# Linear attention, softplus MLP and routed experts on one Trainium2 core: later weight-rest matmuls in an expert unit, and weight conversions held behind attention steps

## The chip, the cores and the metric

One core of one Trainium2 chip. The metric is the device time of one execution in microseconds (us). Engines: PE (TensorE), DVE (VectorE), ACT (ScalarE), POOL (GpSimd), and SP, whose queue issues most DMAs.

## The reference

Three layers in a row, all in float32.

```
q_p, k_p = phi(q), phi(k)                 # phi(x) = exp(x@omega.T - |x|^2/2 - max) / sqrt(m), x scaled
out = (q_p @ (k_p.T @ v)) / (q_p @ sum(k_p) + 1e-6)     # 4 batches, 8 heads, 576 rows, head 64, m = 128
x   = out as 2304 tokens x 512
x   = softplus(x @ w_in) @ w_out          # 512 -> 2048 -> 512
e   = argmax(cosine(x, expert_emb) / tau)  # 8 experts, one per token
out = gate * (relu(x @ w1[e]) @ w2[e])    # 512 -> 1024 -> 512
```

## The kernel before

**Attention** runs in steps (lists `steps` and `loads`, 20 steps for each of 4 batches). Step t transposes one item of q or k (`stage_T`, lines 262 to 270), one step later projects it and takes the exponential (`stage_P`, 282 to 301), and after a lag folds it into the key-value sums (`stage_K`, 318) or turns it for the output (`stage_Q`, 365 to 377). `stage_N`, `stage_M` and `stage_X` (395 to 444) form the quotient and write x. PE, DVE and ACT each have several short instructions in every step. The loads of q and k are issued on SP four steps ahead, those of v one step ahead.

**The MLP** handles 2304 tokens in 6 groups of 384, and d_ff = 2048 in 16 chunks. A chunk is `mm1` (line 638, x times a column block of w_in), the softplus chain on ACT and DVE (653 to 668), and `mm2` (703, times a row block of w_out). Group 0 takes the weights in plain fp32, a chunk's two products in one fp32 matmul each; later groups split each operand into a rounded high part and a rest (fp32r) and make three passes: high by high, rest by high, high by rest. Group 0 starts when attention's first 30 steps are traced (`need[0]=30`); the remaining steps are interleaved with the MLP.

**Weight conversion.** The MLP's weights are loaded in 32 tiles of 512 KB (`load_w`, lines 536 and 540, even n from w_in, odd n from w_out) and turned into scaled values by three DVE instructions each (`conv_ops`, lines 558, 561 and 564). Tiles pass through three staging slots: two of tag `wst`, shared with some router temporaries, and one (`wst3`) for every third tile. `load_w(n + 2)` is called before tile n is converted. `mm1` of chunk f needs tile 2f, `mm2` of chunk f needs tile 2f+1.

**What sets the order.** Up to the first expert unit a planner orders each engine's queue when the kernel is built, from program order and from when it reckons operands and buffers are ready; work that is traced later may so come earlier where an engine would stand idle. On the chip each queue runs in that order. `tc.issue_after(ins)` ties the instructions traced in its block to follow `ins`, on the engine of `ins` alone; here that is DVE, so the loads on SP are not tied. In the kernel before, the loop over the first 30 steps sets the mark only in step 0 (`conv_gate=0`), never converts early (`conv_early=99`), and then calls `conv_to(5)`:

```
    while cur[0] < TUNE["need"][0]:
        if cur[0] >= TUNE["conv_early"] and done_w[0] < 3:
            conv_to(3)
        next(micro)
        if cur[0] <= TUNE["conv_gate"] and traced().engine == mybir.EngineType.DVE:
            marks["conv"] = traced()
    with tc.issue_after(marks["conv"]) if "conv" in marks else ExitStack():
        conv_to(TUNE["conv_first"])
```

**Experts.** Tokens are gathered by expert in slots of 128. A unit (`unit`) is one slot ("single") or two slots with the same expert ("pair"): four singles, then six turns of a pair and a single, then one more single. From unit 1 on the order is written out by hand (`manual_schedule`). While a unit runs, the next one's w1 is split, chunk by chunk c = 0 to 3 (`unit_w1`): ACT writes the high part (line 1246), DVE the rest (line 1250). A single's first product is in two halves of 512 columns (`slot_m1`, line 1336, 12 matmuls of 512 columns each, x stationary); a pair's in four parts k (`pair_m1`, line 1358, 24 matmuls of 256 columns each, w1 stationary). `PASSES` gives the order inside a chunk: high x by high w, high x by rest of w, rest of x by high w. The second product is line 1370.

Of the kernel before, what the change touches and what calls it, by code (L numbers as in the profile page):

```python
# [50 lines left out]
    v_ahead=1,  # L51
    setup=2,
    conv_first=5,
    conv_gate=0,
    conv_early=99,
    gap=0,
    rate=140,
    man=1,
    order='XMTNnKPZ',
# [17 lines left out]
def tile_kernel(ctx, tc, q, k, v, omega, w_in, w_out, emb, tau, w1, w2, out):  # L77
    nc = tc.nc
# [9 lines left out]
    NC = DM // P  # L88
# [1150 lines left out]
    def split(hi, lo, lo_eng, src, relu=False, hi_eng="a"):  # L1239
        if relu:  # L1240
            nc.scalar.activation(out=hi, in_=src, func=AF.Relu)
            nc.vector.scalar_tensor_tensor(out=lo, in0=src, scalar=0.0, in1=hi.bitcast(F32),
                                           op0=ALU.max, op1=ALU.subtract)
        else:
            if hi_eng == "a":
                nc.scalar.copy(out=hi, in_=src)  # L1246
            else:
                (nc.gpsimd if hi_eng == "p" else nc.vector).tensor_copy(hi, src)
            eng = nc.gpsimd if lo_eng == "p" else nc.vector
            eng.tensor_tensor(out=lo, in0=src, in1=hi.bitcast(F32), op=ALU.subtract)  # L1250
# [3 lines left out]
    def mpsum(use, name):  # L1254
        opts = {"t": ("tp", "tp", "kv"), "h": ("h", "pr"), "o": ("y0", "y1", "y2")}[use]
        turns[use] = turns.get(use, -1) + 1
        tag = opts[turns[use] % len(opts)]
        pool = psh if tag == "h" else psy if tag[0] == "y" else psa
        return pool.tile([P, 512], F32, tag=tag, name=name, bufs=2 if tag == "tp" else 1)

    def transposed(src, name):
        pt = mpsum("t", name)
        n = src.shape[1]
        for c in range(n):
            nc.tensor.transpose(pt[:, c * P:c * P + P], src[:, c, :], ident)
        return pt

    xs, w1s, w2s = {}, {}, {}
    PASSES = ((0, 0), (0, 1), (1, 0))

    def unit_x(g):

        n = len(groups[g])
        if n == 2:
            t = [ring.tile([P, 2, 2, P], F32R, tag=f"wi{x}", name=f"mx{x}{k}") for k in range(2) for x in "hl"]
            xs[g] = [[t[2 * (c // 2) + a][:, c % 2] for c in range(NC)] for a in range(2)]
        else:
            if g < NS_A:
                t = [ring.tile([P, NC, P], F32R, tag=f"wi{x}", name=f"mx{x}") for x in "hl"]
            else:  # L1280
                t = xpool.tile([P, 2, NC, P], F32R, tag="xlo", name="mx")
                t = [t[:, 0], t[:, 1]]
            xs[g] = [[x[:, c] for c in range(NC)] for x in t]
        for i, s in enumerate(groups[g]):
            pt = transposed(xgs[s][:, 0:DM].rearrange("t (p c) -> t c p", c=NC), "pt_x")
            pt = pt.rearrange("p (c t) -> p c t", c=NC)
            if n == 2:
                parts = [(t[2 * k][:, :, i, :], t[2 * k + 1][:, :, i, :], pt[:, 2 * k:2 * k + 2]) for k in range(2)]
                for hi, lo, src in parts:
                    nc.scalar.copy(out=hi, in_=src)  # L1290
                for hi, lo, src in parts:
                    nc.vector.tensor_tensor(out=lo, in0=src, in1=hi.bitcast(F32), op=ALU.subtract)
            else:
                split(*t, "v", pt)
# [33 lines left out]
    def slot_m1(g, half, part=slice(0, 12)):  # L1328
        if part.start == 0:
            hs["ps", half] = mpsum("h", "ph")  # L1330
        ph = hs["ps", half]
        w = slice(half * HF, half * HF + HF)
        mms = [(xs[g][a][c], w1s[g, c][b_][:, w]) for c in range(NC) for a, b_ in PASSES]
        for i in range(part.start, part.stop):
            x, r = mms[i]
            nc.tensor.matmul(ph, lhsT=x, rhs=r, start=(i == 0), stop=(i == 3 * NC - 1))  # L1336
# [14 lines left out]
    def pair_m1(g, k):  # L1351

        ph = hs["ps"] = mpsum("h", "ph")
        for c in range(NC):
            for j in range(2):
                f = slice(2 * k * P + j, 2 * (k + 1) * P, 2)
                for n, (a, b_) in enumerate(PASSES):
                    nc.tensor.matmul(ph[:, j * 256:j * 256 + 256], lhsT=w1s[g, c][b_][:, f],  # L1358
                                     rhs=xs[g][a][c].rearrange("p i t -> p (i t)"),
                                     start=(c == 0 and n == 0 and j == 0), stop=(c == NC - 1 and n == 2),  # L1360
                                     skip_group_check=True)

    def unit_m2(g, i, parts):

# [24 lines left out]
    def unit(g):  # L1389
# [22 lines left out]
        if ahead:  # L1412
            fetch_w(g + 2, "1", 1)
        if len(groups[g]) == 2:
            pair_m1(g, 0)
            own(2, 3, 4)
            split(*hidden(0), "v", hs["ps"], relu=True)
            pair_m1(g, 1)
            own(5)
            split(*hidden(1), "v", hs["ps"], relu=True)  # L1420
            pair_m2(g, 0)
            pair_m1(g, 2)
            own(6, 7)
            fetch()
# [7 lines left out]
            if nxt:  # L1432
                unit_x(g + 1)
# [4 lines left out]
        else:  # L1438
            if g > 0:
                slot_m1(g, 0)  # L1440
            own(2, 3, 4)
            slot_relu(0)
            slot_m1(g, 1, slice(0, 5))
            own(5)
            slot_t(0)
            slot_m1(g, 1, slice(5, 12))
            own(6, 7)
            slot_relu(1)
# [4 lines left out]
            if nxt:  # L1453
                unit_x(g + 1)
# [39 lines left out]


    PRE = {TUNE["pre_x"]: [lambda: unit_x(0)]}
    for c in range(NC):
        PRE.setdefault(TUNE["pre_w1"][c], []).append(lambda c=c: unit_w1(0, c))
# [5 lines left out]
    for n in range(NCH):  # L1504
        g, f = divmod(n, NF)
# [22 lines left out]
        if 0 < g < LAST:  # L1528
            t, off = divmod(f - TUNE["y_from"], TUNE["y_step"] if g < LAST - 1 else 1)
# [60 lines left out]
```

## Time and profile before

| what | value |
|---|---|
| median of 3 runs | 950.11 us (948.86 to 951.63) |
| the profiled execution | 950.99 us, span 949.1 us |
| PE busy | 895.0 us (94%) |
| DVE, ACT, POOL busy | 694.6, 651.7, 345.1 us |
| mean granted TensorE clock | 0.991 |

The span is the time from the first to the last instruction in the trace; the execution's own time is 1.9 us more. A share of busy time is a mean over stages: attention alone, attention with MLP group 0, the other MLP groups, the experts. PE's busy time also holds waits inside a matmul group, so it is an upper bound of its work.

### The profile page before, as it was taken

Reading aid. Unit: us, or ns where it says so; the run is one execution under the profiler, and the core shown is the slowest. Engines: PE = TensorE matmul, PEld = TensorE weight load, DVE = VectorE, ACT = ScalarE, POOL = GpSimd, SP = SyncE. Lnnn points to the kernel's source line nnn. Section 1 sums busy time; section 2 is a strip of 40 time slices with the busy share of each in tenths; the row PEclk is TensorE's granted clock in tenths of the full one; section 3 lists DMA queues with packets and bytes.
Section 4 is the critical chain, followed back from the end, with each engine's and each line's share of the span. In section 5 each row is a group of like instructions: output and inputs, shape, how many; then the busy total and the mean of one; then the engine's idle time right before and its main releaser. Section 6 shows DMA issues by size and latency. Waiting matters only on the chain. (4 is left out here: it accounts for less than half of the span.)

```text
span 949.1 us, 14505 instructions
## 1 busy us (share of the span) xinstructions
PE 895.0 (94%) x4951; PEld 743.6 (78%) x4951; DVE 694.6 (73%) x1376; ACT 651.7 (69%) x1452; POOL 345.1 (36%) x341
## 2 busy tenths in 40 slices
PE   7788989999999999999999999999999999999993
PEld 6666545588888879887888889887787887878872
DVE  6698875477888776689886777768967676685762
ACT  4787445477778867776777678876867576585672
POOL 1332400255446654566653110012653242252410
PEclk9999999999999999999999999999999999999997
DMA  4656660011262212010301281102114661451820
GB/s 117 188 170 199 185 180 28 12 39 37 56 147 69 48 47 71 26 40 17 67 7 23 73 331 63 34 12 57 34 56 161 253 240 70 169 211 36 324 86 6
DMA packets 86540, 94.69 MB, mean 100 GB/s; under 512 B 50294, under 2 KB 74870, under 8 KB 84160
## 3 DMA queue, kind: packets, MB, share of 16 engines
q1 hardware_dynamic: 77888, 45.21, 18.4%
q0 software_dynamic: 8576, 48.52, 13.7%
q8 instruction: 41, 0.67, 0.3%
q14 instruction: 35, 0.29, 0.1%
HBM read 108.36 MB, written 15.48 MB: 130 GB/s over the span
## 5 line engine op out<-in xcount | busy, mean ns | idle before, releaser
L1370 PE MATMUL po<-w,mh_h 128*128 128x512 f32 x368 | 116.8, 398 | 0.5 <-ACT mh_h L1347 0.5
L1385 POOL DMA_INDIRECT out_dram<-ot,s_idx x23 | 46.3, 2015 | 166.9 <-ACT ot L1384 126.0
L703 PE MATMUL y<-woh,gh 128*128 128x512 f32 x240 | 97.7, 411 | 3.2 <-DVE gh L682 3.2
L1250 DVE TENSOR_TENSOR w<-w2r,w 128x512 fp32r<-128x512 f32 x136 | 88.2, 687 | 12.3 <-ACT w L1246 12.1
L703 PE MATMUL y<-wol,gh 128*128 128x512 f32 x240 | 94.9, 398 | 0.0
L1246 ACT CAST w<-w2r 128x512 fp32r<-128x512 f32 x136 | 79.4, 643 | 18.4 <-DMA w2r<-in_moe_w_dram,w_idx 9.0
L1250 DVE TENSOR_TENSOR w<-w1r,w 128x1024 fp32r<-128x1024 f32 x68 | 80.3, 1226 | 11.2 <-ACT w L1246 11.2
L703 PE MATMUL y<-woh,gl 128*128 128x512 f32 x240 | 81.5, 406 | 0.4 <-POOL gl L683 0.4
L598 DVE TENSOR_TENSOR wil<-win,wih 128x512 fp32r<-128x512 f32 x72 | 56.9, 790 | 29.2 <-ACT wih L597 25.9
L638 PE MATMUL h<-xhi,wih 128*128 128x384 f32 x320 | 73.6, 349 | 2.8 <-DVE t L657 2.5
L1370 PEld LDWEIGHTS po<-w,mh_h 128*128 128x128 f32 x368 | 66.1, 189 | 12.2 <-ACT mh_h L1347 0.7
L1246 ACT CAST w<-w1r 128x1024 fp32r<-128x1024 f32 x68 | 71.9, 1121 | 3.8 <-PE ph L1336 2.1
L1358 PE MATMUL ph<-mxh,w 128*128 128x256 f32 x384 | 73.0, 286 | 1.4 <-DVE w L1250 0.5
L1370 PE MATMUL po<-w,mh_l 128*128 128x512 f32 x184 | 72.6, 395 | 1.7 <-DVE mh_l L1349 1.7
L425 POOL TENSOR_TENSOR xf<-xf,rc 128x256 f32<-128x256 f32 (+1 forms) x20 | 19.9, 994 | 143.7 <-ACT rc L424 129.0
L638 PE MATMUL h<-xlo,wih 128*128 128x384 f32 x320 | 71.9, 340 | 0.0
L638 PE MATMUL h<-xhi,wil 128*128 128x384 f32 x320 | 69.6, 337 | 0.0
L1358 PEld LDWEIGHTS ph<-mxh,w 128*128 128x128 f32 x384 | 62.7, 195 | 5.1 <-DVE w L1250 3.8
L610 POOL TENSOR_TENSOR wol<-wout,woh 128x512 fp32r<-128x512 f32 x40 | 54.2, 1355 | 27.8 <-ACT woh L609 24.9
L638 PEld LDWEIGHTS h<-xhi,wih 128*128 128x128 f32 x320 | 55.1, 188 | 7.6 <-DVE t L657 3.0
L638 PEld LDWEIGHTS h<-xhi,wil 128*128 128x128 f32 x320 | 57.5, 188 | 0.0
L638 PEld LDWEIGHTS h<-xlo,wih 128*128 128x128 f32 x320 | 56.5, 188 | 0.5
(311 smaller groups left out, 2415.1 us busy)
## 6 DMA issues: line engine op xcount, KB each, us to landing
wst<-in_moe_w_in_dram SPq DMA_DIRECT2D x16, 512.0 KB, 3.9
wst<-in_moe_w_out_dram SPq DMA_DIRECT2D x16, 512.0 KB, 3.7
raw<-in_k_dram SPq DMA_DIRECT2D x32, 128.0 KB, 2.3
vf<-in_v_dram SPq DMA_DIRECT2D x64, 64.0 KB, 2.2
raw<-in_q_dram SPq DMA_DIRECT2D x32, 128.0 KB, 2.3
ya<-yt SPq DMA_DIRECT2D x20, 128.2 KB, 3.9
yb<-yt SPq DMA_DIRECT2D x20, 128.2 KB, 3.6
ya<-yt SPq DMA_DIRECT2D x8, 256.5 KB, 4.7
```

The costliest lines, as they stand in the source:

```text
L425: nc.gpsimd.tensor_tensor(out=xf, in0=xf, in1=rc, op=ALU.mult)
L598: feng("il", n).tensor_tensor(out=il, in0=wi, in1=ih.bitcast(F32), op=ALU.subtract)
L610: feng("ol", n).tensor_tensor(out=ol, in0=wo, in1=oh.bitcast(F32), op=ALU.subtract)
L638: nc.tensor.matmul(h[:, 0:G], lhsT=a[:, c, :], rhs=x[:, c, :], start=(i == 0), stop=(i == last))
L703: nc.tensor.matmul(y, lhsT=x[:, c], rhs=w, start=(f == 0 and i == 0), stop=(f == NF - 1 and i == len(passes) - 1))
L1246: nc.scalar.copy(out=hi, in_=src)
L1250: eng.tensor_tensor(out=lo, in0=src, in1=hi.bitcast(F32), op=ALU.subtract)
L1358: nc.tensor.matmul(ph[:, j * 256:j * 256 + 256], lhsT=w1s[g, c][b_][:, f], rhs=xs[g][a][c].rearrange("p i t -> p (i t)"), start=(c == 0 an ...
L1370: nc.tensor.matmul(po[s], lhsT=h[a][:, o:o + P], rhs=w2s[g, c][b_], start=(c == 0 and n == 0), stop=(c == 7 and n == 2))
L1385: nc.gpsimd.indirect_dma_start(out=out, out_offset=bass.IndirectOffsetOnAxis(ap=s_idx[:, s:s + 1].bitcast(U32), axis=0), in_=ot, in_offset ...
```

## The change

Two edits. `first_order` puts, in the first half of a single's first product and in the first part of a pair's, the matmuls with the rest of w1 behind all the others; the other parts keep their order by chunk, but a pair's parts now run through the two column halves j inside a pass. And the mark is now set by every step up to 29, tiles 0 to 2 are converted from step 8 on, and tiles 3 and 4 (`conv_to(5)`) are tied to the mark.

```
-    conv_gate=0,
-    conv_early=99,
+    conv_gate=29,
+    conv_early=8,
...
+    def first_order(part):
+        if part == 0:
+            return [(c, p) for c in range(NC) for p in ((0, 0), (1, 0))] + [(c, (0, 1)) for c in range(NC)]
+        return [(c, p) for c in range(NC) for p in PASSES]
...
-        mms = [(xs[g][a][c], w1s[g, c][b_][:, w]) for c in range(NC) for a, b_ in PASSES]
+        mms = [(xs[g][a][c], w1s[g, c][b_][:, w]) for c, (a, b_) in first_order(half)]
...
-        for c in range(NC):
+        order = first_order(k)
+        for n, (c, (a, b_)) in enumerate(order):
             for j in range(2):
                 f = slice(2 * k * P + j, 2 * (k + 1) * P, 2)
-                for n, (a, b_) in enumerate(PASSES):
-                    nc.tensor.matmul(ph[:, j * 256:j * 256 + 256], lhsT=w1s[g, c][b_][:, f],
-                                     rhs=xs[g][a][c].rearrange("p i t -> p (i t)"),
-                                     start=(c == 0 and n == 0 and j == 0), stop=(c == NC - 1 and n == 2),
-                                     skip_group_check=True)
+                nc.tensor.matmul(ph[:, j * 256:j * 256 + 256], lhsT=w1s[g, c][b_][:, f],
+                                 rhs=xs[g][a][c].rearrange("p i t -> p (i t)"),
+                                 start=(n == 0 and j == 0), stop=(n == len(order) - 1), skip_group_check=True)
```

## Rows read from the trace of the kernel before

**Rows 1.** Windows by stage, all engines: length, then busy us (instructions), PE clock, DMA.

```profile
0.00:28.00 28.00, 22.36 (x154) 20.22 (x155) 19.83 (x45) 14.52 (x37) 4.15 (x34) 1.00 0.47 120
28.00:84.00 56.00, 43.04 (x274) 34.10 (x274) 48.35 (x94) 44.22 (x139) 22.81 (x22) 0.97 0.67 195
84.00:150.00 66.00, 62.04 (x245) 36.59 (x245) 54.40 (x120) 31.01 (x83) 10.46 (x13) 1.00 0.54 165
```

**Rows 2.** Line 558, the first DVE instruction of each conversion, in the same stretches.

```profile
0.00:28.00 28.00, 0.00 (x0) 1.00 0.47 120
28.00:84.00 56.00, 8.40 (x13) 0.97 0.67 195
84.00:150.00 66.00, 8.32 (x19) 1.00 0.54 165
```

**Rows 3.** DVE in order of time, 32 to 40 us: start, length, line, tile, idle before.

```profile
32.01 0.69 DVE L288 TENSOR_REDUCE nm<-pp 128x4 f32<-128x512 f32 x1
35.16 0.43 DVE L558 TENSOR_SCALAR win<-wst 128x512 int32<-128x512 int32 x1 [2.46 <-DMA wst<-in_moe_w_in_dram]
...
38.84 0.43 DVE L558 TENSOR_SCALAR wout<-wst 128x512 int32<-128x512 int32 x1 [1.78 <-DMA wst<-in_moe_w_out_dram]
39.18 0.68 DVE L288 TENSOR_REDUCE nm<-pp 128x4 f32<-128x512 f32 x1
39.78 0.68 DVE L564 SCALAR_TENSOR_TENSOR win<-wst,win 128x512 int32<-128x512 int32 x1
```

**Rows 4.** ACT in order of time at 39.9 us.

```profile
39.90 1.14 ACT L301 ACTIVATE kl<-pp,nm 128x128 f32<-128x128 f32 x4 [3.54 <-DVE nm L288]
```

**Rows 5.** What PE waited for, 28 to 50 us: total, times, longest.

```profile
PE kv L318 <- ACT kh L301: 2.4, 2, 1.7
PE nd L395 <- ACT kh L301: 2.0, 1, 2.0
PE pt_q L365 <- ACT pe L301: 1.8, 1, 1.8
```

**Rows 6.** A window of 36 to 42 us, columns as in group 1.

```profile
36.00:42.00 6.00, 5.67 (x29) 4.86 (x30) 4.22 (x12) 2.46 (x10) 1.58 (x2) 0.72 0.72 207
```

**Rows 7.** What PE waited for, 0 to 28 us, longest.

```profile
PE om_ps L222 <- DMA om<-in_omega_dram: 3.1, 1, 3.1
```

**Rows 8.** Waits of line 558 over the whole span; landing times of the staging loads.

```profile
DMA wst<-in_moe_w_out_dram: 8.3, 7
DMA wst<-in_moe_w_in_dram: 6.2, 6
DMA to landing us min/median/max: 3.4/3.9/6.8
```

**Rows 9.** Group 0's second product: count, duration min/median/max, first and last start.

```profile
L703 PE MATMUL y<-wout,gf x96: 592/592/697, 88.2 to 193.8; 128*128 128x512 f32 x96
```

**Rows 10.** PE, ACT and DVE around a single unit's first half, in order of time.

```profile
714.59 3.90 ACT L1246 CAST w<-w1r 128x1024 fp32r<-128x1024 f32 x4
715.67 4.63 DVE L1250 TENSOR_TENSOR w<-w1r,w 128x1024 fp32r<-128x1024 f32 x4 [0.25 <-ACT w L1246]
718.09 0.98 PE L1336 MATMUL ph<-w,mx 128*128 128x512 f32 x3 [0.18 <-DVE w L1250]
719.22 0.96 PE L1336 MATMUL ph<-w,mx 128*128 128x512 f32 x3 [0.16 <-DVE w L1250]
720.36 1.90 PE L1336 MATMUL ph<-w,mx 128*128 128x512 f32 x7 [0.17 <-DVE w L1250]
```

**Rows 11.** PE at the end of a pair's first part.

```profile
734.05 0.39 PE L1358 MATMUL ph<-mxh,w 128*128 128x256 f32 x1 [0.16 <-DVE w L1250]
734.28 0.29 PE L1358 MATMUL ph<-mxl,w 128*128 128x256 f32 x1
734.41 0.40 PE L1358 MATMUL ph<-mxh,w 128*128 128x256 f32 x2
734.65 0.28 PE L1358 MATMUL ph<-mxl,w 128*128 128x256 f32 x1
```

## The prediction, made before the change was run

> **What bounds the kernel now.** I read the windows by stage first. While attention runs alone with the weight conversions beside it, PE works 43.0 of 56 us and DVE 48.4; in the stretch behind it, where MLP group 0 has begun, PE works 62.0 of 66 [rows 1]. So PE is nearly full once the MLP runs, and its free time ahead of that is 13.0 us in one stretch and 4.0 in the next. Second, where the conversions lie: 13 of 32 begin in the first of these stretches, 19 in the second, none earlier [rows 2]. Third, DVE in order of time. It finishes a maximum at 32.0, then stands 2.46 us before a conversion whose tile has not landed and, a little later, 1.78 us before the next; attention's next maximum, queued behind, starts only at 39.18 [rows 3]. ACT stood 3.54 us for it [rows 4], and PE's waits on ACT from 28 to 50 us come to 6.2 us [rows 5]. There a conversion in DVE's queue sets PE's pace. The clock shows it too: behind the idle time, from 36 to 42 us, the granted clock is 0.72 of 2.4 GHz, a mean of the two levels 1.2 and 2.4 [rows 6]. Last, the expert units: there PE waits in a unit's first part, chunk by chunk, for DVE's rests of w1 [rows 10].
>
> **The change, part by part.** The sum is made against the profiled execution (950.99 us, span 949.1), which is 0.9 us above the median of 950.11.
>
> *Rests at the end.* No instruction is added or removed, so the cost as such is nothing. In the single shown, the four rests take DVE from 715.67 to 720.30, 1.16 us a chunk, and PE starts chunk c's second matmul as each lands, the last at 720.36 [rows 10]. Moving the rests back does not make the last rest earlier, and no first part can end before it: the gain is only what PE still had to do behind it. Before, that is two matmuls (rest, then low x); now it is one. From that group of seven, (1.90 - 0.39) / 6 = 0.25 us each. The high parts do not bind instead: they are done at 718.49, and six matmuls behind that end at 719.99, ahead of the last rest [rows 10]. In a pair five matmuls stood behind the last rest's arrival at 734.05; in the new order two stand (rest for j = 0 and 1). The three saved are worth about 0.12 us each (0.40 for two against 0.28 for one) [rows 11]. Six singles show this pattern and six pairs do: 6 x 0.25 + 6 x 0.36 = 3.7 us. The chain behind (relu, transposes, next unit's w1, which waits for PE's transposes of x) starts earlier by as much, so the gains add up. Bounds: 0, if the next unit's fetches hold the loop, and 3.7.
>
> *Attention freed of conversions.* In 28 to 84 us, 10 of the 13 conversions move behind step 29. Three DVE instructions each (0.43, 0.75 and 0.68 us [rows 2, 3]; the middle one has no row of its own, so I take 0.68) make 1.8 us, 18 us of DVE in all. What PE then needs: 43.0 us of work, less 5.67 x 0.28 = 1.6 us lost to the slower clock [rows 6], is 41.4. How full can PE be in attention alone? In the first 28 us, which have no conversion, it idles 5.6 us, 3.1 of them for the first load [rows 1, 7]: 2.5 of 24.9, 10%. So 41.4 / 0.9 = 46.0 us in place of 56: a gain of 10.0. Bounds: 0 (ACT, at 44.2 us of 56 [rows 1], is then the pace) and 14.6 (no idle).
>
> *Three early tiles.* They and their loads move to step 8. By the code a step issues one to three loads on SP; now three to five of 512 KB stand ahead of attention's. The conversions' 5.4 us fit into DVE's 8.2 free us of the first stretch [rows 1]. But DVE's queue is in order, and if a tile is late everything behind stands as at 35 and 38 us. That cost 2.46 + 1.78 = 4.2 us of DVE [rows 3]; it may come again or not, so I take half, 2.1 (bounds 0 and 6.2, PE's own waits [rows 5]).
>
> *Group 0.* It starts some 10 us earlier with 3 tiles in hand, and 29 conversions must run beside it instead of 19. PE's free time there was 4.0 us [rows 1]; by the number of tiles 4.0 x 29 / 19 = 6.1, so 2.1 more. The stock is also gone: the fourth tile's successor in its slot must land (median 3.9 us [rows 8]) with little cover, so I add half a landing, 2.0. Behind the waiting conversion in DVE's queue stand the softplus sum (line 668), for which `mm2` waits, and attention's maxima. Bounds for both together: 0 and 8. The loads of tiles 3 and 4 aren't tied and cost nothing: they land under attention; without that cover each costs a landing.
>
> The sum: 3.7 + 10.0 - 2.1 - 2.1 - 2.0 = 7.5 us. 950.99 - 7.5 = 943.5 for an execution like the profiled one, 942.6 against the median. From there on PE is 94 to 100% busy or tied to its own earlier work, so what is won in front stays won.
>
> **The rivals.** *ACT holds attention.* The exponentials, copies and quotients give ACT 44.2 us in that stretch, more than PE's 43.0 [rows 1]; the 10% of the first 28 us come from steps with fewer output stages, where ACT worked only 14.5 of 28. Then the 56 us stay, only the rests' 3.7 us are won and group 0 gives back the 2.1: 950.1 - 1.6 = 948.5, from 946.5 to 951. Against it: ACT's own longest wait was on DVE [rows 4].
>
> *Conversions starve group 0: slower.* The place is DVE's queue from 74 us on (84 less the 10 won). Before, tiles came every 66 / 19 = 3.5 us [rows 1, 2], with waits on their loads of 14.5 us in 13 places over the span [rows 8]. The last tile is needed some 6 us before the last second product, which starts at 193.8 [rows 9], so at about 188. It decides from (188 - 74) / 29 = 3.9 us a tile. At 3.5 the last one comes at 74 + 101 = 175, in time; at 4.2, with three slots that refill one landing later, at 196, 8 us late: 950.1 + 8 - 3.7 = 954.
>
> *The clock falls in group 0.* After the idle time near 35 us the granted clock was 0.72 for 6 us, which cost 1.6 us [rows 6]. If PE waited so in each of group 0's later 14 chunks, that is 14 x 1.6 = 22 us: near 970. The Trainium skill ("TensorE: Matmul & The Clock Gate", on HAM oscillation) says that a loop in which PE stands for each round's load starts every round at half clock; the trace agrees in one place, where the clock fell behind such a wait. But the stretch of 84 to 150 us shows 1.00 throughout, with its 4.0 us of gaps [rows 1]: 2%.
>
> *The change holds less than it says.* Only instructions traced inside the block are tied: tiles 3 and 4. The next two in the `wst` slots are held by these, but tile 5 uses the third slot, free after tile 2, and 8 and 11 follow in it. If the planner moves these three forward, 7 tiles leave the stretch instead of 10: 3 of the 10 us are lost, 945.6.
>
> **How the numbers follow.** About 0.3% (2.85 us) is what a measurement can tell from no change here, so faster is below 947.3, slower above 953.0. Forecast, 936 to 947: 0.50. Holds less, 943 to 948: 0.14. ACT holds attention: 0.22, a quarter of it below 947.3. Starved: 0.12, and the clock 0.02. Faster: 0.49 + 0.13 + 0.06 = 0.68. Same: 0.01 + 0.01 + 0.15 = 0.17. Slower: 0.01 + 0.12 + 0.02 = 0.15. The range runs from 936 (950.1 - 3.7 - 10.0, no give-back) to 951.5: beyond it lie the starved and slow-clock cases, 0.14, and some 0.04 below.
>
> **What would show it.** Right: three conversions before 30 us, then none until step 29's transposed rest (line 270, 30th) at about 74; group 0's last second product starts near 188; in the units a DVE-paced half ends one matmul after its last rest, with PE's two earlier waits gone. Wrong: conversions of tiles 5, 8, 11 ahead of step 29; PE waits on the softplus sum or on a converted tile of more than 8 us in group 0; the stretch up to step 29 as long without conversions as with them; units with the same distance as before, so that something else sets their pace.

## The result, and the profile after

The changed kernel takes 941.71 us (median of 5 executions, 938.91 to 943.80) against 951.19 us (5 executions, 948.86 to 952.02): a ratio of 0.990, 95% interval 0.988 to 0.992, 9.5 us by the medians. The profiled execution took 942.76 us (span 940.9), 8.2 us less than before's 950.99. Forecast was 942.6 us, a gain of 7.5, range 936 to 951.5. The total is right. Its parts are not: by the end of MLP group 0 a third of what was forecast for the early stages was left, and more than was missing came from a place that the change doesn't touch.

The windows by stage, columns as in [rows 1]; the fourth stretch is the rest of group 0:

```profile
0.00:28.00 28.00, 19.72 (x124) 17.65 (x125) 19.40 (x47) 12.19 (x29) 5.13 (x35) 0.92 0.64 176
28.00:84.00 56.00, 49.56 (x328) 40.56 (x328) 40.12 (x82) 51.39 (x159) 17.86 (x22) 0.98 0.42 110
84.00:150.00 66.00, 60.78 (x238) 35.17 (x236) 58.15 (x126) 28.63 (x74) 9.08 (x15) 1.00 0.61 191
150.00:194.00 44.00, 43.13 (x161) 25.90 (x160) 24.62 (x46) 20.96 (x49) 7.67 (x11) 1.00 0.16 48
```

Against [rows 1], PE works 6.5 us more in the second stretch (49.56 for 43.04), 2.6 less in the first, where the clock in this execution is 0.92, and 1.3 less in the third. DVE has turned over: 8.2 us less busy in attention, 3.8 more beside group 0, where it is now at 58.15 of 66. ACT is the fullest engine of attention alone, 51.39 of 56.

Line 558 in the first three stretches, answering [rows 2]:

```profile
0.00:28.00 28.00, 1.69 (x4) 0.92 0.64 176
28.00:84.00 56.00, 2.53 (x3) 0.98 0.42 110
84.00:150.00 66.00, 9.86 (x22) 1.00 0.61 191
```

The conversions lie where the prediction put them: three tiles before 30 us, none until step 29's transposed rest at 73.75 (the fourth line 558 before 28 us is the first instruction of tile 3, traced ahead of the held block), the rest behind it. Next, the first stretch in order of time, the lines that answer to [rows 3]:

```profile
18.32 0.43 DVE L558 TENSOR_SCALAR win<-wst 128x512 int32<-128x512 int32 x1 [2.08 <-DMA wst<-in_moe_w_in_dram]
...
19.22 0.36 PE L282 MATMUL pp<-obd_hi,xThi 128*128 128x256 f32 x1 [0.88 <-DVE pe L296]
...
22.21 0.44 PE L266 MATMUL pt_q<-ident,raw 128*128 128x128 f32 x2 [1.55 <-DMA raw<-in_q_dram]
...
24.55 0.55 PE L282 MATMUL pp<-obd_hi,xThi 128*128 128x256 f32 x1 [1.25 <-DVE pe L296]
```

DVE's wait for a tile that has not landed did not go; it moved from 35 us to 18 us, 2.08 for 2.46. PE waits behind it, then for a load of q that was issued at 16.8 us, behind the three loads of 512 KB (from 13.7), then for DVE again. From 28 to 50 us the waits of [rows 5] shrink to 1.2 (line 318) and 0.9 us (line 395). From 36 to 42 the clock is 1.00 where [rows 6] has 0.72, but that alone is no gain of the change: two more executions with before's order in this stretch, among the runs below (only the last chunk's rest moved, and the gate's exponential moved), also show 1.00 there.

Where group 0 starts, 73.7 to 79 us, all engines in order of time:

```profile
73.75 0.42 DVE L270 TENSOR_TENSOR xTlo<-pt_k,xThi 128x256 fp32r<-128x256 f32 x1
...
74.22 1.27 POOL L425 TENSOR_TENSOR xf<-xf,rc 128x320 f32<-128x320 f32 x1 [2.04 <-ACT rc L424]
...
74.69 1.09 DVE L558 TENSOR_SCALAR win<-wst 128x512 int32<-128x512 int32 x1
...
77.92 0.28 DVE L433 SCALAR_TENSOR_TENSOR x<-den,xf 128x128 f32<-128x128 f32 x1
...
78.25 0.91 PE L638 MATMUL h<-x,win 128*128 128x384 f32 x2 [0.61 <-DVE x L433]
```

Group 0's x is complete only at 78.2: its last product stands in DVE's queue behind the conversions that were let go at 73.75. Six of the eight matmuls of chunk 0's first product have started by then, from 72.92 us on; the last two wait for it, 0.61 us. Group 0's second product, which answers to [rows 9], and then what DVE waited for from 84 to 150 us (total, times, longest):

```profile
L703 PE MATMUL y<-wout,gf x96: 592/592/697, 87.0 to 195.4; 128*128 128x512 f32 x96
```

```profile
DVE wout L558 <- DMA wst<-in_moe_w_out_dram: 3.5, 6, 1.4
DVE win L558 <- DMA wst<-in_moe_w_in_dram: 3.3, 7, 1.2
```

The last second product starts at 195.4, 1.6 us later than in [rows 9]; forecast was 188. DVE's 58.15 busy us and 6.8 of waiting for tiles fill 65 of the 66 us. PE's waits there are led by the softplus sum (line 668): three of them, 3.4 us in all, against 2.8 before.

Last, a single's first part, which answers to [rows 10] (the new function shifts the lines: 1343 and 1376 here are 1336 and 1370 before):

```profile
709.60 3.90 ACT L1246 CAST w<-w1r 128x1024 fp32r<-128x1024 f32 x4
...
710.68 4.63 DVE L1250 TENSOR_TENSOR w<-w1r,w 128x1024 fp32r<-128x1024 f32 x4 [0.25 <-ACT w L1246]
...
713.55 1.43 PE L1343 MATMUL ph<-w,mx 128*128 128x512 f32 x5 [0.21 <-ACT w L1246]
...
715.37 1.66 PE L1343 MATMUL ph<-w,mx 128*128 128x512 f32 x6 [0.39 <-DVE w L1250]
```

The rests end at 710.68 + 4.63 = 715.31, the last matmul of the part starts at 715.37, and the second half follows without a pause; of PE's three waits on DVE in [rows 10] one is left.

**PE's work by time.** To compare runs whose orders differ, I add up the matmuls started by a given time, each at the pitch from start to start that is usual for its kind in these traces (the 30th percentile). The table gives the difference to before in us (positive: more done); it is worked out from the starts, and is no line of a trace. Every trace holds the same 4951 matmuls. The last column is the start of the 30th line 270, step 29; that moment also depends on how many matmuls of group 0 the queues put ahead of it (10 before, 3 in the changed kernel).

```
run                           28 us  84 us  194 us 345 us 360 us 632 us | step 29
before                          0      0      0      0      0      0    | 83.72
changed kernel                -4.4   +3.8   +1.2   +1.1   +4.8   +5.7   | 73.75
hold and early tiles, no rests-4.0   +3.5   -0.7   +0.2   +3.4   +4.2   | 74.07
hold, no early tiles          +0.5   +5.8   -3.8   -2.4   +0.2   +1.0   | 68.00
early tiles, no hold          -4.7   -1.9   -1.1   -1.0   -1.1   -1.4   | 90.05
early tiles at step 13        -2.2   +3.2   -0.4   -0.4   +2.8   +3.6   | 74.33
x first                       -4.6   +5.0   -1.2    0.0   +2.8   +3.5   | 74.16
five tiles let in             -4.5   +2.6   -1.1   -6.0   -3.4   -2.4   | 80.26
early loads apart             -0.6   +7.0   +3.1   +4.1   +7.7   +6.9   | 72.31
early loads apart, tile 5 held-0.9   +6.1   -2.0   -0.9   +1.9   +2.7   | 72.28
before's order up to the units:
  rests alone                 -3.0   -1.6   -1.7   -1.8   -0.2   -4.0   | 86.15
  last rest only              -0.8   +0.3   +0.7   +0.9   +1.5   +1.1   | 83.26
before's order up to 356 us:
  gate's exponential later    +0.4   +1.0   +1.2   +1.3   +3.1   +2.1   | 82.67
the change's order up to the units:
  one rest of four on POOL    -4.1   +4.5   +1.3   +1.5   +5.0   +5.9   | 73.18
```

The last four rows tell how far single traces scatter. Ahead of the units, the rests alone and the last rest only have the same instructions in the same order as before on PE, DVE, ACT and POOL. Yet the rests alone lie 3.0 us behind by 28 us, where PE waited 2.4 us for a load of k and the clock was 0.91, and 4.0 by 632. The change's order, with three traces (the changed kernel, the hold and the early tiles alone, one rest on POOL), agrees to 2.0 us in every column. So a difference of 1 or 2 us, or in a few places of 3, between two rows can be the execution alone.

The changed kernel's row tells where the time came from: -4.4 by 28 us, +8.2 to 84, -2.6 to 194, nothing to 345, **+3.7 between 345 and 360**, +0.9 after that. Then the units: from the first second product of unit 1 to that of the last single it takes 267.40 us instead of 271.24, 3.8 less; 1.3 us are lost at 638 to 642 us, where this execution's clock is 0.57.

### The profile page after: what moved, and what is told of

Read it like the earlier page. It is cut to its first block, busy times and chain, and to the rows that moved or that the text cites. A ratio compares the mean times of both kernels' runs of the same rounds, so it can differ in the third digit from the quotient of the medians.

```text
span 940.9 us, 14526 instructions
## 1 busy us (share of the span) xinstructions
PE 891.9 (95%) x4951; PEld 744.5 (79%) x4951; DVE 689.8 (73%) x1376; ACT 652.8 (69%) x1452; POOL 323.0 (34%) x341
## 3 DMA queue, kind: packets, MB, share of 16 engines
q0 software_dynamic: 8576, 48.52, 13.7%
## 5 line engine op out<-in xcount | busy, mean ns | idle before, releaser
L1391 POOL DMA_INDIRECT out_dram<-ot,s_idx x23 | 31.5, 1369 | 171.0 <-ACT ot L1390 126.5
L610 POOL TENSOR_TENSOR wol<-wout,woh 128x512 fp32r<-128x512 f32 x40 | 55.0, 1376 | 45.3 <-ACT woh L609 45.2
L1365 PE MATMUL ph<-mxh,w 128*128 128x256 f32 x384 | 62.6, 285 | 0.4
L425 POOL TENSOR_TENSOR xf<-xf,rc 128x256 f32<-128x256 f32 (+1 forms) x20 | 17.3, 867 | 122.0 <-ACT rc L424 114.8
L1365 PEld LDWEIGHTS ph<-mxh,w 128*128 128x128 f32 x384 | 55.0, 195 | 2.9 <-ACT w L1246 1.6
```

The source lines that it names most:

```text
L425: nc.gpsimd.tensor_tensor(out=xf, in0=xf, in1=rc, op=ALU.mult)
L610: feng("ol", n).tensor_tensor(out=ol, in0=wo, in1=oh.bitcast(F32), op=ALU.subtract)
L1391: nc.gpsimd.indirect_dma_start(out=out, out_offset=bass.IndirectOffsetOnAxis(ap=s_idx[:, s:s + 1].bitcast(U32), axis=0), in_=ot, in_offset ...
```

## The experiments

Each run was timed beside the kernel before on the same chip (949.99, 950.57, 951.14 and 950.57 us in the four sessions); a ratio is to that.

### The rests alone

```
kernel before, with first_order() in slot_m1 and pair_m1 as in the change
```

> The kernel before with the rests of w1 moved to the end of a unit's first part, and the conversions as before. My theory (a first part ends only one matmul instead of two, in a pair two instead of five, behind its last rest; 6 x 0.25 + 6 x 0.36 us): 3.7 us faster, between 2.5 and 4.5; group 5's last second product at the same time as before (637.7 us, within 1), and a turn of a pair and a single 0.6 us shorter than the 38.2 us of before. Rival (what the expert units win comes from their meeting the conversions' change, or from an order of the queues that changes ahead of them too): less than 1.5 us, or a shift of more than 2 us already at group 5's end.

948.22 us (11 executions), ratio 0.9969 (0.9957 to 0.9981): 2.9 us by the ratio, 1.8 by the medians, where at least 2.5 was expected. Unit 1 to the last single is 3.4 us shorter. That is no accident of two traces: the five traces with the rests where they were take 270.8 to 271.2 us from unit 1 to the last single, the eight with the rests or the last rest at the end (one rest on POOL left out) 267.4 to 267.9. One sign that the expectation gave to the rival did show: group 5's last second product starts at 641.8 us in this trace, 4.1 later than before. But the order on PE, DVE, ACT and POOL up to the units is before's, so this is the execution and not the rival's other order: it took 952.39 us, the longest of the 11, with a mean clock of 0.984.

### The hold and the early tiles alone

```
-    conv_gate=0,
-    conv_early=99,
+    conv_gate=29,
+    conv_early=8,
```

> The kernel before with the two settings of the conversions alone (mark up to step 29, three tiles from step 8), the units as before. If the edits are independent: 949.1 - 940.9 = 8.2 us of span less the units' 3.4, so 4.8 us faster, all of it ahead of group 5's end. By the account of PE's work in the changed kernel, about 1 us of it is won by the end of group 0 and the rest from 300 to 425 us. Rival (the gain of 300 to 425 us is an accident of the queues' order and not of the hold): the same order ahead of the units, so this run alone can't refute it; but a run with the same settings whose middle does not gain would show that the middle hangs on something else: then 0 to 1.5 us faster.

945.12 us (4 executions), ratio 0.9937 (0.9914 to 0.9959). The product of the two ratios is 0.9906, the change's 0.9898 (0.9879 to 0.9918): the two edits add up.

### Only the last chunk's rest moved

```
+            return [(c, p) for c in range(NC - 1) for p in PASSES] + [(NC - 1, p) for p in ((0, 0), (1, 0), (0, 1))]
```

> The kernel before, with only the fourth chunk's rest moved to the end of a unit's first part; the first three chunks' rests stand where they stood and the conversions are as before. Theory: a first part cannot end before its last rest has landed, so only what PE has to do behind that rest counts, and here that is the same as with all rests at the end (one matmul instead of two in a single, two instead of five in a pair). Expected: the whole gain of the run with all rests at the end, 3 us of the time (2 to 4), the distance of a pair and a single shorter by 0.5 to 0.6 us, with PE's waits for the earlier rests still there. Rival: the waits for the earlier rests cost time too. Then about a third of the gain: 1 us (0 to 1.5), a turn shorter by about 0.2 us.

948.12 us (10 executions), ratio 0.9975 (0.9951 to 0.9999); unit 1 to the last single 3.4 us shorter, as with all rests moved. PE's waits on a w1 rest in singles, from 655 to 930 us, before and then in this run (total, times, longest):

```profile
PE ph L1336 <- DVE w L1250: 3.2, 19, 0.2
```

```profile
PE ph L1343 <- DVE w L1250: 2.1, 12, 0.2
```

Twelve waits remain, and the gain is the same 3.4 us as with all rests moved: the part ends with its last rest in any case. The theory stands; the rival (a third of the gain) falls.

### The hold without the early tiles

```
-    conv_gate=0,
+    conv_gate=29,
```

> The hold without the three early tiles: all five tiles that are converted ahead of group 0 are tied behind step 29; units as before. My theory: the early tiles cost 4.4 us of PE's work by 28 us (in the changed kernel), which is not paid here, and attention's step 29 comes at 68 to 71 us instead of 74; but group 0 then starts with no tile and waits for the first conversions, 1.8 us a tile and more, so that 3 to 5 us are given back: 3 to 7 us faster than before, within 2.5 of the run with early tiles. Rival (the early tiles are what lets group 0 start early): group 0's first product ends at 82 us or later, and the time is no better than before.

949.52 us (10 executions), ratio 0.9988 (0.9972 to 1.0004): a miss. Step 29 comes at 68.00, as expected, 15.7 us earlier than before, and then DVE converts three tiles side by side. It is busy for all of the 10 us from 68 to 78. PE, whose next steps of attention stand behind them in DVE's queue, is busy for 7.37 of the 10, at a clock of 0.83:

```profile
68.00 0.42 DVE L270 TENSOR_TENSOR xTlo<-pt_k,xThi 128x256 fp32r<-128x256 f32 x1
...
71.64 0.47 PE L330 MATMUL pt_z<-ident,kvs 65*128 65x65 f32 x4 [2.07 <-ACT kvs L252]
...
73.90 0.68 DVE L564 SCALAR_TENSOR_TENSOR win<-wst,win 128x512 int32<-128x512 int32 x1
...
75.11 0.68 DVE L564 SCALAR_TENSOR_TENSOR win<-wst,win 128x512 int32<-128x512 int32 x1
...
77.71 2.75 PE L638 MATMUL h<-x,win 128*128 128x384 f32 x8
```

Group 0's last second product starts at 200.0, 6.2 us later than before. Without the early tiles the hold does not pay, although by themselves they cost.

### The early tiles without the hold

```
-    conv_early=99,
+    conv_early=8,
```

> The three early tiles without the hold: mark in step 0 only, units as before. My theory: attention's steps pay for the early tiles and again for the conversions in between, so step 29 comes no earlier than before (82 to 88 us), while group 0 has more tiles in hand: 0 to 4 us slower than before, at most 1 faster. Rival (what counts is that weights are ready early): 3 us or more faster.

951.37 us (10 executions), ratio 1.0008 (0.9996 to 1.0021). Step 29 at 90.05, later than expected. With the run above this prices both edits on attention, twice each: the hold takes 15.7 us off step 29 without the early tiles (83.72 to 68.00) and 16.3 with them (90.05 to 73.75); the early tiles add 6.3 without the hold and 5.8 with it. Not all of this is attention's: matmuls of group 0's first products stand ahead of step 29, 10 of them before, none with the hold alone, 16 with the early tiles alone and 3 in the changed kernel. At 2.75 us for eight (an estimate from the lines above), the hold takes 12.3 and 11.8 us off attention, and the early tiles add 4.3 and 4.7. Each is the difference of two single traces, and step 29 alone scatters from 82.67 to 86.15 us with before's order.

### The early tiles at step 13

```
-    conv_early=8,
+    conv_early=13,
```

> The changed kernel, with the three early tiles (loads and conversions) at step 13 instead of step 8; all else the same. Theory: the 4 to 5 us that the changed kernel loses in its first 28 us come of loads of 512 KB ahead of attention's first loads and of the half clock behind that wait, so later they cost less: PE's step 9 back near 21 to 22 us, step 29 at 70 to 72, the time 1 to 3 us below the changed kernel's. Rival: the cost moves with them (three conversions and three loads hold attention by as much at step 13 as at step 8): step 29 at 73 to 75, the time within 1 us of the changed kernel's.

940.65 us (4 executions), ratio 0.9883 (0.9839 to 0.9926), level with the change. Step 9's transposed rest starts at 20.70 instead of 26.12, but step 29's at 74.33. The rival holds: the cost moves along with the three loads and conversions.

### x ahead of the conversions

```
+        if any(x[0] == 0 for x in (x_pieces(b, half) if b == 0 else ())):
+            marks["x0"] = traced()
...
+    with tc.issue_after(marks["x0"]):
         conv_to(TUNE["conv_first"])
```

> The changed kernel, with the held conversions tied to the last product of group 0's x (the 128 wide one that writes x) instead of to step 29's last DVE instruction. In the changed kernel that product stands in DVE's queue behind five conversion instructions and lands at 78.2 us, and group 0's first product waits for it. Theory: this wait is part of what group 0 gives back. Expected: x near 75.5, the first product of group 0 ends 2 to 3 us earlier, the fourth conversion 1 to 3 us later, group 0's end 0 to 2.5 us earlier and the time 0 to 2.5 us below the changed kernel's. Rival: from 74 us on the conversions are the pace, so what x wins the second chunk loses: first product earlier, but the second chunk's first product and all behind it later by 1 to 3 us, the time 0 to 3 us above the changed kernel's.

944.38 us (9 executions), ratio 0.9939 (0.9913 to 0.9966). The first products of chunks 0 to 2 are 1.3, 3.1 and 4.8 us earlier than in the changed kernel, and from the second product of chunk 4 on (119.82 for 118.56) all of group 0 is later, its end at 197.5. The rival holds, and its reason fits: DVE's queue is the pace there, and what x wins the conversions lose. How much is not shown by this trace alone, since PE also ran at half clock from 116.2 to 119.6 us in it. The wait at 78.25 was not had back by this order.

### Five of the held tiles let into attention

```
-    conv_first=5,
+    conv_first=9,
...
+    spread={15: 4, 18: 5, 21: 6, 24: 7, 27: 8},
...
+            n = TUNE["spread"].get(cur[0], 0)
+            if done_w[0] < n:
+                with tc.issue_after(marks["conv"]):
+                    conv_to(n)
```

> The changed kernel, but five of the held conversions are let into attention one at a time, each tied to DVE's last instruction of its step: the fourth tile behind step 15, then 18, 21, 24 and 27; the rest behind step 29. Theory: what cost attention time was DVE standing for tiles that had not landed and several conversions in a row, not their mean work; from 28 to 74 us DVE is idle for some 16 us and five conversions of 1.9 us fit singly. Expected: step 29's transposed rest no more than 1.5 us later than in the changed kernel (73.75), eight or nine conversions done by then, group 0's last second product 2 to 4 us earlier than its 195.4, the time 1.5 to 4 us below the changed kernel's. Rival: each conversion in attention costs it about 1 us wherever it stands (10 us for 10). Then step 29 comes at 78 to 79, group 0 ends where it did, and the time is within 1.5 us of the changed kernel's.

950.13 us (10 executions), ratio 0.9987 (0.9966 to 1.0008): a miss. Step 29 comes at 80.26, as the rival has it, yet by 84 us the run is only 1.2 us of work behind the changed kernel. Most of its loss, 5.1 us, falls between 194 and 300 us, where no conversion is left: there the queues' order differs, and why this order is worse was not followed further.

### The early loads taken apart

```
-    conv_early=8,
+    early={7: (1, 0), 10: (2, 1), 13: (3, 2), 16: (3, 3)},
```

The pairs are the loads issued and the tiles converted by the end of a step; the loop and the changes to `conv_all` that follow them are not shown.

> The changed kernel, with the three early tiles' loads and conversions taken apart: one load at step 7, 10 and 13 each, and each tile converted three steps behind its load, tied behind DVE's last instruction of that step; the rest behind step 29 as it is. Theory: the 4.4 us that the changed kernel loses in its first 28 us come of DVE standing 2.1 us for a tile that has not landed, of three loads of 512 KB in a row ahead of attention's, and of the half clock behind PE's wait; with loads one at a time and a stock of landed tiles none of the three remains. Expected: PE's step 9 at 21 to 23 us instead of 26.1, step 29 at 70 to 72.5 instead of 73.75, the time 1 to 3 us below the changed kernel's. Rival: what costs is the conversions' and loads' share as such, wherever they stand in the first 45 us (the run that moved them to step 13 won nothing): step 29 at 73 to 75, the time within 1 us of the changed kernel's or above it.

940.90 us (4 executions, 938.51 to 942.82), ratio 0.9891 (0.9855 to 0.9926): not to be told from the changed kernel by its time. The trace does part them: the first stretch loses 0.6 us of work instead of 4.4, with a clock of 1.00, step 9 at 21.32, step 29 at 72.31, and by 194 us 3.1 us are won. So a part of the early tiles' cost was the order of loads and waits; not all, as step 29 still comes 4.3 us later than without early tiles (68.00), 3.3 without the three matmuls of group 0 that stand ahead of it. Also, two of the three conversions now fall behind the first stretch. Tiles 5, 8 and 11 left the hold here: in the changed kernel `conv_to(3)` runs one instruction ahead, so that tile 5's first one is traced inside the held block; in this run it isn't.

### The same with tile 5 held

```
-    conv_first=5,
+    conv_first=6,
```

> The run with the early loads taken apart, with one more tile inside the held block (tiles 3, 4 and 5 instead of 3 and 4). In that run tiles 5, 8 and 11, whose own slot was free, were converted at 50.7, 60.1 and 66.1 us, ahead of step 29, as the rival of the prediction 'the change holds less than it says' has it; here they stay behind it. Theory (the prediction's price, 1 us of attention for each conversion): step 29 at 69 to 70 instead of 72.3, and the time 1 to 3 us below the run with the loads taken apart, 2 to 4 us below the changed kernel's. Rival: three conversions 6 to 9 us apart cost attention next to nothing and are a stock that group 0 lives on: step 29 at 71.5 to 72.5, group 0's last second product later than that run's 191.1, the time level with it or up to 2 us above.

944.84 us (5 executions, 943.77 to 945.66), ratio 0.9938 (0.9924 to 0.9951), slower than the run without it: the executions of the two do not overlap, though they are of two chips and the intervals of the ratios just touch. From 28 to 84 us 6 tiles begin here and 9 there. Group 0's second product, of the run above and then of this one:

```profile
L704 PE MATMUL y<-wout,gf x96: 592/592/697, 83.4 to 191.1; 128*128 128x512 f32 x96
```

```profile
L704 PE MATMUL y<-wout,gf x96: 592/592/1061, 84.3 to 198.3; 128*128 128x512 f32 x96
```

Three conversions 6 to 9 us apart leave step 29 where it was (72.31 and 72.28; the first is 1.1 us later when the 3 and 6 matmuls of group 0 ahead of it are taken out), and without them group 0 ends 7.2 us later. Not all of the 7.2 us is the missing stock: this execution twice ran at half clock in group 0, from 133.3 to 136.7 and from 146.9 to 150.4 us, which is worth at most half of these 6.9 us.

```profile
84.00:150.00 66.00, 58.09 (x205) 32.67 (x204) 53.32 (x120) 24.75 (x62) 10.28 (x13) 0.95 0.59 188
```

The rival holds: these conversions cost some 0.4 us each and not 1, although DVE stood 1.63 us (at 50.67) and 0.51 us (at 66.12) for the tiles of two of them. Why three early ones in a row cost more, whether for their number, their loads or their place, is not shown.

### The stretch from 345 to 360 us

The windows of before, then of the changed kernel (columns as in group 1):

```profile
300.00:345.00 45.00, 43.95 (x278) 38.98 (x277) 34.99 (x58) 38.15 (x107) 32.08 (x31) 1.00 0.22 42
345.00:360.00 15.00, 12.97 (x76) 11.33 (x76) 11.85 (x24) 8.70 (x25) 8.16 (x8) 0.89 0.43 103
```

```profile
300.00:345.00 45.00, 44.08 (x282) 38.49 (x281) 36.79 (x67) 37.92 (x101) 31.84 (x31) 1.00 0.19 44
345.00:360.00 15.00, 15.00 (x94) 13.72 (x93) 11.30 (x17) 10.31 (x25) 7.31 (x8) 1.00 0.55 150
```

And before in order of time, 347 to 351 us:

```profile
348.06 0.89 DVE L971 TENSOR_TENSOR d<-d,sq 128x24 f32<-128x24 f32 x1
...
348.98 0.22 ACT L973 ACTIVATE ex<-d 128x24 f32<-128x24 f32 x1 [3.43 <-DVE d L971]
...
349.23 0.38 ACT L401 ACTIVATE den<-nd 64x256 f32<-64x256 f32 x1
...
349.62 0.37 ACT L252 COPY xf<-nd 64x256 f32<-64x256 f32 x1
...
350.04 0.81 PE L395 MATMUL nd<-qT1hi,kzh 128*128 128x320 f32 x2 [2.03 <-ACT xf L252]
```

A small exponential of the router's gate stands at the head of ACT's queue for 3.43 us; the copy behind it frees the buffer that PE's next quotient needs, and PE stands 2.03 us and then runs from 351 to 355 at a clock of 0.57. The wait belongs to the order; the half clock belongs to that execution. With the same order the rests alone and the last rest only show the same wait (2.00 us in both) and a clock of 1.00 for the whole stretch. Their windows, in this order:

```profile
345.00:360.00 15.00, 13.01 (x86) 11.68 (x84) 11.45 (x25) 9.47 (x25) 7.90 (x9) 1.00 0.38 92
345.00:360.00 15.00, 12.30 (x77) 10.43 (x75) 12.18 (x25) 8.24 (x23) 7.28 (x8) 1.00 0.53 134
```

With the hold, attention is further ahead of the MLP: measured against the end of group 0, step 59 comes some 7.8 us earlier than before in every run with the hold but one (early loads apart, 3.2), and at most 0.2 earlier in the runs without (rests alone, early tiles alone). The queues are then ordered otherwise there, and all nine traces with the hold (the changed kernel's among them) gain 2.6 to 3.7 us of work in this stretch; of those without, the early tiles alone lose 0.1, one rest alone gains 0.6 and all rests 1.6, which that execution loses again by 425 us. So what the hold wins here is 2 to 3 us against a typical trace, and 3.7 against the trace of before. To test the place of the exponential itself, it was moved one chunk later in the kernel before, and with it all that follows from it in the gate (the sum, the reciprocal, the stores), which is not shown:

```
-        nc.scalar.activation(out=ex, in_=d, func=AF.Exp)
+        with tc.issue_after(marks["ln"]) if g == 1 else ExitStack():
+            nc.scalar.activation(out=ex, in_=d, func=AF.Exp)
```

> The kernel before, with one thing moved: the small exponential of the router's gate for the second token group (the line that ACT reached at 345.5 us and stood 3.4 us for) is held behind the softplus logarithm of a later chunk. Conversions and rests are as before. The changed kernel wins 4.7 us between 300 and 425 us that nobody asked of it. Theory: that is the place of this exponential against attention's steps in ACT's queue; before, it holds ACT, ACT's copy comes late, PE stands 2.0 us for it and runs at half clock for 3.4 us behind that. Expected: the kernel before without PE's 2.0 us wait at 348 and with a granted clock of 1.00 from 345 to 360 us, 2.5 to 4 us won by 360 us; if nothing else in the order behind it costs, the time 2 to 4 us below before. Rival: another instruction holds PE there whatever stands in ACT's queue, or the order that follows from the move loses it again elsewhere: PE's wait of 1 us or more remains between 340 and 360 us, and the time is within 1.5 us of before.

949.75 us (10 executions), ratio 0.9990 (0.9975 to 1.0005). The stretch, in this run:

```profile
345.00:360.00 15.00, 14.08 (x89) 11.57 (x88) 11.97 (x20) 8.23 (x24) 7.11 (x8) 1.00 0.17 43
```

PE's wait of 2.03 is gone (0.19 is left at its matmul), and 1.8 us of work are won from 345 to 360; by 425 us 1.2 of them are lost again. So the exponential's place did cost the wait. The 1.8 us are little more than the 1.6 that the rests alone show with the exponential in its old place, and taking the wait away alone does not carry to the end: the rival's part on the whole time holds. That the change's gain here is due to the new order is shown by the runs with and without the hold, 2.6 or more in each of nine against 1.6 or less (1.8 with the exponential moved); which of its many moves carries it is open.

### One rest of four on POOL

```
-    w1=['vvvv', 'vvvv', 'vvvv'],
+    w1=['vvvv', 'vpvv', 'vpvv'],
```

> The changed kernel, with the second chunk's rest of w1 computed by POOL instead of DVE in the pairs and the later singles; chunks one, three and four stay on DVE. Theory: a first part ends one matmul behind its last rest, so with three rests on DVE instead of four the last lands about 1.1 us earlier, until the high parts bind, 0.4 us earlier than now: 0.3 to 0.4 us for each of 12 units, the time 3 to 5 us below the changed kernel's. Rival: POOL's operation of 128 by 1024 takes some 2.8 us (1.4 us for 128 by 512 in group 2) and slows DVE beside it by about as much as it relieves it (1.09 instead of 0.43 us were seen for a conversion beside POOL), so the last rest lands no earlier: the time from 1 us below to 8 us above the changed kernel's.

959.56 us (4 executions), ratio 1.0088 (1.0058 to 1.0119), 18 us above the changed kernel, worse than the rival's bound. From 745 to 800 us:

```profile
752.69 1.23 DVE L1250 TENSOR_TENSOR w<-w1r,w 128x1024 fp32r<-128x1024 f32 x1 [0.25 <-ACT w L1246]
...
753.69 2.48 POOL L1250 TENSOR_TENSOR w<-w1r,w 128x1024 fp32r<-128x1024 f32 x1 [11.00 <-ACT w L1246]
...
754.59 3.80 DVE L1250 TENSOR_TENSOR w<-w1r,w 128x1024 fp32r<-128x1024 f32 x2 [0.67 <-ACT w L1246]
```

The first of DVE's two rests, beside POOL's, takes 2.67 us, and the second 1.21; alone one takes 1.22. The last rest so ends 5.7 us after DVE's first starts (752.69 to 758.39), where four on DVE need 4.63, and the part ends later with it. From unit 1 to the last single it takes 285.49 us instead of 267.40, which is all of the 18.

## Why the prediction was right, and where not

**Rests at the end: right.** 3.7 us forecast from the matmuls behind the last rest; 3.4 in the trace with the rests alone, 3.8 in the changed kernel, 2.9 by the ratio of the times and 1.8 by their medians. The run with one rest moved shows the mechanism: only what stands behind the last rest counts.

**Attention freed of conversions: right in kind, too small.** Forecast 10.0 us, bounds 0 and 14.6; the hold alone takes 15.7 off step 29, some 12 without group 0's matmuls. The fullness taken, 0.9, was about right (PE 29.55 of 34 us, 0.87, from 28 to 62 us in the run with the hold alone). The step that failed is "what PE then needs: 41.4": in that run PE is busy for 35.0 us from 28 us to step 29. The forecast counted the ten matmuls of group 0 as attention's, some 3.4 us, and PE's busy time, which also holds waits inside a matmul group, as work; that the latter makes up the rest is not shown. (Its 0.75 us for a conversion's middle instruction stands in no row; the sum took 0.68, which is what the traces show, 0.69 at 74.09 us.) The rival that ACT holds attention at 56 us falls, but ACT is the next limit: it is busy for 31.50 of those 34 us, more than PE, and for 51.39 of 56 in the changed kernel.

**Three early tiles: the sign right, the size not.** 2.1 us forecast as half of 4.2; they cost 5.8 to 6.3 us of step 29, 4.3 to 4.7 without group 0's matmuls, and 4.4 us of work by 28 us, inside the bound of 6.2. "It may come again or not": it came again in full, and with it a late load of q and a clock of 0.92, which the sum had no term for. (The rests alone, without early tiles, show a late load and 0.91 there once too; the seven traces with three early tiles in a row lie 2.1 to 4.7 us behind before by 28 us, the four others without early tiles from 3.0 behind to 0.5 ahead.) The two errors offset each other, which is luck: step 29 comes 10.0 us earlier (83.72 to 73.75), 7.6 without group 0's matmuls, and forecast was 10.0 - 2.1 = 7.9.

**Group 0: wrong.** Forecast was that 4.1 of the 7.9 us are given back and that its last second product starts near 188; it starts at 195.4. The work won in attention was attention's own; group 0 could not follow, since DVE had 29 tiles to finish beside it and was full. Of the 3.8 us ahead at 84 us, 2.6 are given back by 194: 1.2 us are left of a forecast 3.8. The place was named (DVE's queue, the softplus sum, 3.4 us of PE's waits), the price was too low.

**"What is won in front stays won": wrong, to the good.** 4.5 us more are won between 194 and 632 us, 3.7 of them from 345 to 360; the two other traces with the change's order there win 4.6 and 4.9. The step failed by taking the order of the queues behind group 0 as given. The planner derives it anew from the whole program; without this windfall, by an estimate from these rows, the change would have won some 5 us. That the total met the forecast to within 1 us is luck.

**The rivals.** *Conversions starve group 0*: no; the last conversion ends at 159.97 and the fourth at 77.39, so 2.9 us a tile, below the deciding 3.9. *The clock falls in group 0*: 1.00 from 84 to 150 us, in spite of 5.2 us of gaps. The Trainium skill ("TensorE: Matmul & The Clock Gate", on HAM oscillation) expects half clock round after round where PE waits for each round's load; the changed kernel's trace does not show it in group 0. Single falls do come there in other runs: one with x ahead of the conversions (116.2 us), two with tile 5 held (133.3 and 146.9). The prediction took before's fall at 37.4 us as what such a wait brings. The runs show that it need not: near 350 us the same wait of 2.0 us was followed by half clock in before and with the early tiles alone, and by full clock with the rests alone and with the last rest only. *The change holds less than it says*: it did not, by the accident of one instruction traced ahead; and where it did (early loads apart) the result was better than with tile 5 held, so the rival had its sign wrong too. *ACT holds attention*: no.

## What to carry to other kernels

Work moved off an engine that sets the pace of one stage arrives in the next; look first whether that engine is free there (before the change DVE was already busy for 54 of 66 us and waited 9.3 for tiles). Moving it apart can be better than moving it away: by two single traces, conversions that came 6 to 9 us apart cost attention some 0.4 us each and left group 0 a stock, while three in a row, right behind their loads, cost 4 to 5 us. It is no rule: in another run five tiles let into attention one by one undid nearly all of the gain, 5.1 us of it between 194 and 300 us, behind the last conversion. And where a planner derives the queues' order, an edit moves the order of stages that it never names, by some microseconds either way: compare work done by time, not only the end, before a gain is put down to the edit's reason, and compare it in more than one execution of the same order, to see how far that measure scatters.

## What the runs showed of the hardware

POOL can slow DVE. Line 558 took 0.43 us alone and 1.09 beside POOL's lines 425 and 426 (74.69 us), but not each time: at 27.06 us it took 0.42 with POOL's line 610 on record beside it all along. A rest of 128 by 1024 took 1.22 us alone and 2.4 to 2.7 beside POOL's, which itself took 2.4 to 2.5. The Trainium skill ("GPSIMD Engine Reference", Specifications) says that GpSimd's SBUF interfaces are shared with VectorE, with contention for instructions with two SBUF inputs or in a two-port mode; the rests have two inputs and agree; line 558 has one, and no run here shows its mode or why POOL slowed it at one time and not at another.

Executions of one kernel differ by the clock they are granted: the changed kernel's five have spans of 937.0 us at a mean clock of 0.994, 939.2 at 0.993, 939.8 at 0.990, 940.9 at 0.990 and 941.9 at 0.988. A difference of 2 us between two profiles can be that alone, which is why single profiles are compared here by stretch and the times by medians. Where the clock falls also differs between executions of one order: before shows half clock from 37.4 to 40.8 and from 351.4 to 354.9 us, the rests alone from 23.2, 50.5, 364.6 and 647.9 us instead, and the last rest only nowhere between 9.4 and 934 us.
